# Sigmoid attention in turns of two head pairs, with the last 64 keys of four heads computed in quarters of the PE array

## The chip, the cores and the metric

The kernel runs on one core of a Trainium2 chip. The metric is the device time of one execution in microseconds (us). Before the change three runs took 1089.77, 1091.10 and 1091.86 us; the median is 1091.1 us. The profile shows one more execution, which took 1089.6 us.

## The reference

Three layers run one behind the other. The first is the attention, with a sigmoid in place of the softmax; the change is there alone.

```python
# 1. attention: batch 4, 12 heads, 448 rows, head width 64
scores = (1/sqrt(64)) * (q @ k.T) - log(448)        # 448 x 448 for every head
x = sigmoid(scores) @ v                             # heads side by side: 4 x 448 x 768
# 2. gated layer
h = relu(x @ w_in)                                  # 768 -> 1024
u, v = h[..., :512], h[..., 512:]
v_n = (v - mean(v)) / sqrt(var(v) + 1e-6)
gated = u * (einsum('ts,bsd->btd', w_spatial, v_n) + b_spatial)
x = gated @ w_out                                   # 512 -> 768
# 3. MLP
xn = (x - mean(x)) / sqrt(var(x) + 1e-6) * g_ln
out = x + relu(xn @ w_ch1) @ w_ch2                  # 768 -> 3072 -> 768
```

## The kernel before, in words

**Numbers.** Everything is fp32. Most matmuls take each operand as a high and a low part in the type fp32r and add three products (high with high, high with low, low with high), each of which goes through the PE once. The sums over v in the attention are plain fp32 matmuls instead; each of them shows as two records in the trace.

**Attention.** The 48 heads are taken as 24 pairs. A pair's q and k lie transposed in SBUF, the first head in partitions 0 to 63 and the second in 64 to 127. `qk_load` (L347) fetches them raw, `qk_split` (L363) makes the high and low parts: two casts on the VectorE and two subtractions on GpSimd (the first two pairs aside). A pair has four blocks of 128 keys. The last block has 64 keys of its own: the host repeats the last 64 keys to fill it up to 512 and sets the repeated rows of v to zero, so that half of its work adds nothing. `qk` (L377) computes two blocks of scores: per block six matmuls with 64 rows and 128 columns of the array each, in three twos, one head of the pair in the upper half of the array's rows and the other in the lower half; a block lands in two PSUM banks, one for each head, out of a pool of two such double banks (`ps2`). The ScalarE makes the sigmoid of a block in one instruction (L391). `av` (L394) sums over two blocks: per block two fp32 matmuls, 128 rows and 64 columns of the array each, one head in the left half of the columns, the other in the right half. `x_end` (L407) splits the pair's result into the next layer's operand x (ScalarE copy, VectorE subtraction), and frees the bank.

**The order.** It is written out by hand in the loop of L735. A step is half a pair. Even steps: two blocks of scores (blocks 0 and 1 of pair p), then the sums of the whole pair p-1 (16 records). Odd steps: two blocks of scores (2 and 3), then a stretch of background matmuls worth 2 * BG_US = 4.6 us by the kernel's own costs. The background (`bg`, L724) computes the gated layer's first matmuls `hv` and `hu` for the batches 0 to 2, lines 246 to 248; it does nothing as long as its x or its weights are not there. After each step `jobs.pop` runs one or two jobs of the weight pipeline: `load` of a chunk of w_in (768 KB), `decode` (ScalarE L265, VectorE L266, L267, L270), `split` (ScalarE L276, VectorE L277). There are two raw buffers for chunks, so the load of chunk n+2 waits for the decode of chunk n. All loads go through SyncE's queue in order, but for a few at the start.

**Memory.** Raw q and k have rings of three buffers, their parts rings of two, sigmoids a ring of six. PSUM has the two double banks and four single banks (`ps1`), which the sums and the background share.

**After the attention** w_spatial is loaded (L766) and split (`w_split`, L807), and the last batch's `hv` and `hu`, the spatial matmuls, the projection and the MLP follow.

Of the kernel before, what the change touches and what calls it, by code (L numbers as in the profile page):

```python
# [10 lines left out]
F32 = mybir.dt.float32  # L11
F32R = mybir.dt.float32r
U32 = mybir.dt.uint32
AF = mybir.ActivationFunctionType
ALU = mybir.AluOpType

P = 128
B, H, S, D = 4, 12, 448, 64
NPAIR = H // 2
SK = 512  # L20
DM = H * D
KC = DM // P
DFF = 1024
# [17 lines left out]
BG_US = 2.3  # L41
# [8 lines left out]
VN_DVE = [range(4), range(4), (1, 3), (1, 3)]  # L50
HU_EVERY = 3

PLAIN = range(B * H)

R_SIZE, F_SIZE = 34944, 17664

# [85 lines left out]
class Ring:  # L142
# [61 lines left out]
def sigmoid_attention_gmlp_mlp(ctx: ExitStack, tc, q, k, v, w_in, w_sp, w_out, g_ln, w1, w2, out):  # L204
    nc = tc.nc
# [1 line left out]
    small = ctx.enter_context(tc.tile_pool(name="small", bufs=4))  # L207
    dram = ctx.enter_context(tc.tile_pool(name="dram", bufs=1, space=bass.MemoryType.DRAM))
    ps_s = ctx.enter_context(tc.tile_pool(name="ps_s", bufs=2, space=bass.MemoryType.PSUM))
    ps_1 = ctx.enter_context(tc.tile_pool(name="ps_1", bufs=4, space=bass.MemoryType.PSUM))  # L210

    R = Arena("r", const.tile([P, R_SIZE], F32R, name="r_all"))
    F = Arena("f", const.tile([P, F_SIZE], U32, name="f_all"))
# [6 lines left out]
    bias_s = const.tile([P, 1], F32, name="bias_s")  # L220
# [12 lines left out]

    ctx.enter_context(tc.manual_schedule())

    def ps1():
        return ps_1.tile([P, 512], F32, tag="ps1", name="ps1")

    def ps2():
        return ps_s.tile([P, 2, 512], F32, tag="ps2", name="ps2")  # L240
# [77 lines left out]
    now = [0]  # L318
# [6 lines left out]
    wu = [R.alloc(KC * DH), R.alloc(KC * DH)]  # L325
    xp = [R.alloc(KC * 2 * S), R.alloc(KC * 2 * S)]
    q_r = [Ring(R, S, 2) for _ in range(2)]
    k_r = [Ring(R, SK, 2) for _ in range(2)]
    rv = Ring(F, 512, 3)
    rq = Ring(F, S, 3)  # L330
    rk = Ring(F, SK, 3)
    af_r = Ring(F, 2 * S, 6)
    a_rings = [*q_r, *k_r, rv, rq, rk, af_r]

    n_pairs = B * NPAIR
    pairs = {}
# [9 lines left out]
    @on_pairs  # L346
    def qk_load(p, b, hp):  # L347

        qr, kr = rq.next().ap(S), rk.next().ap(SK)
        pairs[p] = dict(raw=(qr, kr))  # L350
        for j in range(2):
            rows = slice(D * j, D * j + D)
            eng = nc.scalar if p < 3 and j else nc.sync
            eng.dma_start(kr[rows], k[b, hp, :, j])  # L354
            eng.dma_start(qr[rows], q[b, hp, :D, j])

    @on_pairs
    def pv_load(p, b, hp):
        pairs[p]["v"] = rv.next().ap(8, D)
        nc.sync.dma_start(pairs[p]["v"], v[b, hp])  # L360

    @on_pairs
    def qk_split(p, b, hp):  # L363
        t = pairs[p]
        qr, kr = t["raw"]
        (qh, ql), (kh, kl) = ([r.next().ap(n) for r in rs] for rs, n in ((q_r, S), (k_r, SK)))
        t.update(qh=qh, ql=ql, kh=kh, kl=kl)
        eng = nc.gpsimd if p > 1 else nc.vector
        if p:
            nc.vector.tensor_copy(kh, kr)  # L370
        else:
            nc.scalar.copy(kh, kr)
        nc.vector.tensor_copy(qh, qr)
        eng.tensor_sub(kl, kr, kh)  # L374
        eng.tensor_sub(ql, qr, qh)  # L375

    def qk(p, t):  # L377


        a = pairs[p]  # L380
        for c in (2 * t, 2 * t + 1):
# [8 lines left out]
            af = af_r.next().ap(2, S)  # L390
            nc.scalar.activation(af, ps[:, :, :S], AF.Sigmoid, bias=bias_s, scale=1.0 / math.sqrt(D))  # L391
            a["a", c] = af

    def av(p, t):  # L394

        a = pairs[p]
        if t == 0:
            a["ps"] = ps1()
        for c in (2 * t, 2 * t + 1):
            af = a.pop(("a", c))  # L400
            for j in range(2):
                rows = slice(D * j, D * j + D)
                nc.tensor.matmul(  # L403
                    a["ps"][rows, :S], a["v"][:, 4 * j + c], af[:, j], start=(c == 0), stop=(c == 3)
                )
# [41 lines left out]
    def hv(b):  # L447
# [281 lines left out]
    qk_load(1)  # L729
    pv_load(0)  # L730
    qk_split(0)
    qk_load(2)
    pv_load(1)
    jobs.pop(1)
    for i in range(2 * n_pairs):  # L735
        p, t = divmod(i, 2)
        now[0] = i
        qk(p, t)
        if t == 0:
            qk_split(p + 1)  # L740
            qk_load(p + 3)
        else:
            pv_load(p + 2)
        if t:
            bg.run(2 * BG_US)
        elif p:
            av(p - 1, 0)
            av(p - 1, 1)
            x_end(p - 1)
        jobs.pop(0 if i < FIRST else 2 if i >= MORE else 1)  # L750
        if i == WO_FROM:
            c0, c1, c2, c3 = wo_chunks
            for job in (c0.load, c1.load, idle, c0.decode, c1.decode, c2.load, c3.load):
                jobs.add([job, idle])
    now[0] += 1
    av(n_pairs - 1, 0)
    av(n_pairs - 1, 1)
    x_end(n_pairs - 1)
    now[0] = 10**9
    for r in a_rings:  # L760
        r.free()

    wsp_b = R.at(PLACE_WSP, 8 * S)
    wsp = wsp_b.cut(4 * S, 4 * S)
# [157 lines left out]
```

## Time and profile before

| | us |
|---|---|
| median of three runs | 1091.1 (1089.77 to 1091.86) |
| the profiled execution | 1089.6 |
| its span, first to last instruction | 1087.4 |
| PE busy | 1074.3 (99%) |
| VectorE, ScalarE, GpSimd busy | 542.0, 315.6, 104.3 |
| score matmuls L387, 576 records | 73.7 |
| sums L403, 384 records | 77.5 |
| sigmoids L391, 96 | 91.4 |

PE is the matmul part of TensorE, PEld its loading of weights, DVE the VectorE, ACT the ScalarE, POOL GpSimd, SP SyncE (SPq: its issuing of DMAs). A busy time counts overlapping instructions once. Matmul records overlap: the distance from start to start tells what one costs, the length of a record does not. The attention fills the first 247 us.

### The profile page before, as it was taken

How to read it: one execution, taken by the hardware profiler on the slowest of the kernel's cores; microseconds unless marked ns; L12 is line 12 of the kernel's file. 1: busy time of each engine (PE TensorE's matmuls, PEld its weight loads, DVE VectorE, ACT ScalarE, POOL GpSimd, SP SyncE). 2: the span in 40 equal slices, each digit the busy share in tenths (PEclk: the TensorE clock that was granted, in tenths of full speed). 3: DMA queues.
4: the chain of work that ended last, by engine and by line, in shares of the span. 5: the costliest groups of instructions: out<-in, count | busy, mean ns of one | idle time of the engine just before them, and what ended most of it. 6: DMA issues, size and time to landing. Idle time of an engine off the chain costs nothing.

```text
span 1087.4 us, 14037 instructions
## 1 busy us (share of the span) xinstructions
PE 1074.3 (99%) x5860; PEld 877.6 (81%) x5860; DVE 542.0 (50%) x789; ACT 315.6 (29%) x465; POOL 104.3 (10%) x96
## 2 busy tenths in 40 slices
PE   7999999999999999999999999999999999999998
PEld 4466666668888888888888888888888888888887
DVE  4750113205676866364555555463636464555533
ACT  6764445443543432111212121211212111212110
POOL 1232121211215510000000000000000000000000
PEclk9999999999999999999999999999999999999999
DMA  9743335315510112011111112020202011111013
GB/s 244 218 125 96 98 107 173 123 61 189 180 65 1 59 59 88 30 58 58 59 59 58 59 34 83 9 80 30 87 30 87 30 59 58 58 58 58 1 58 145
DMA packets 31951, 87.94 MB, mean 81 GB/s; under 512 B 7568, under 2 KB 12816, under 8 KB 31760
## 3 DMA queue, kind: packets, MB, share of 16 engines
q1 hardware_dynamic: 29808, 78.97, 22.5%
q0 software_dynamic: 1600, 7.34, 2.0%
q8 instruction: 46, 0.75, 0.3%
q10 hardware_dynamic: 480, 0.74, 0.2%
q14 instruction: 17, 0.14, 0.0%
HBM read 74.17 MB, written 12.86 MB: 80 GB/s over the span
## 4 chain that ended last, share of the span: by engine, by line
PE 92%; issue 5%; DMA 1%; POOL 1%; ACT 0%; DVE 0%; SPq 0%; POOLq 0%; DVEq 0%
PE ps L246 27%; PE ps L247 26%; PE ps L248 26%; PE ps L403 6%; PE ps L387 5%; DMA f_all<-in_q 1%; PE ps L597 1%; DMA f_all<-in_k 0%; POOL vnorm L420 0%; POOL r_all L375 0%; PE ps L537 0%; PE ps L536 0%; POOL f_all L778 0%; DVE f_all L539 0%; SPq L354 0%
## 5 line engine op out<-in xcount | busy, mean ns | idle before, releaser
L246 PE MATMUL ps<-r_all 128*128 128x512 f32 (+2 forms) x1588 | 562.9, 354 | 2.3 <-DVE f_all L539 1.1
L247 PE MATMUL ps<-r_all 128*128 128x512 f32 (+2 forms) x1588 | 559.8, 352 | 0.0
L248 PE MATMUL ps<-r_all 128*128 128x512 f32 (+2 forms) x1588 | 557.9, 351 | 0.0
L246 PEld LDWEIGHTS ps<-r_all 128*128 128x128 f32 x1588 | 300.3, 189 | 50.3 <-issue 6.9
L248 PEld LDWEIGHTS ps<-r_all 128*128 128x128 f32 x1588 | 299.7, 189 | 39.4
L247 PEld LDWEIGHTS ps<-r_all 128*128 128x128 f32 x1588 | 300.4, 189 | 37.5
L652 DVE TENSOR_TENSOR f_all<-ps,f_all 128x768 f32<-128x768 f32 (+1 forms) x169 | 161.1, 953 | 164.4 <-PE ps L248 164.3
L634 ACT ACTIVATE r_all<-ps 128x512 fp32r<-128x512 f32 (+1 forms) x96 | 52.0, 542 | 393.2 <-PE ps L248 393.2
L635 DVE SCALAR_TENSOR_TENSOR r_all<-ps,r_all 128x512 fp32r<-128x512 f32 (+1 forms) x96 | 59.7, 622 | 144.5 <-ACT r_all L634 144.5
L391 ACT ACTIVATE f_all<-ps,bias_s 128x896 f32<-128x896 f32 x96 | 91.4, 1003 | 40.0 <-PE ps L387 39.7
L276 ACT CAST r_all<-f_all 128x768 fp32r<-128x768 f32 x60 | 49.8, 834 | 172.5 <-DVE f_all L270 137.1
L277 DVE TENSOR_TENSOR r_all<-ps,r_all 128x384 fp32r<-128x384 f32 (+1 forms) x52 | 29.1, 582 | 127.3 <-ACT r_all L276 127.3
L387 PE MATMUL ps<-r_all 64*128 64x448 f32 x576 | 73.7, 383 | 6.3 <-ACT f_all L391 4.0
L387 PEld LDWEIGHTS ps<-r_all 64*128 64x128 f32 x576 | 50.3, 184 | 36.2 <-issue 20.8
L403 PE MATMUL ps<-f_all 128*64 128x448 f32 x384 | 77.5, 545 | 0.0
L277 DVE TENSOR_TENSOR r_all<-f_all,r_all 128x768 fp32r<-128x768 f32 x60 | 58.0, 970 | 16.2 <-ACT r_all L276 16.2
L267 DVE SCALAR_TENSOR_TENSOR f_all<-f_all 128x768 uint32<-128x768 uint32 x60 | 57.5, 958 | 2.1
L270 DVE SCALAR_TENSOR_TENSOR f_all<-f_all 128x768 uint32<-128x768 uint32 x60 | 57.5, 958 | 2.1
L403 PEld LDWEIGHTS ps<-f_all 128*64 128x64 f32 x384 | 25.4, 136 | 40.9 <-issue 40.0
L265 ACT ACTIVATE f_all<-f_all 128x768 f32<-128x768 f32 x60 | 54.4, 906 | 5.1 <-DVE r_all L277 5.1
L374 POOL TENSOR_TENSOR r_all<-f_all,r_all 128x512 fp32r<-128x512 f32 x22 | 30.1, 1370 | 166.5 <-DVE r_all L370 153.6
L266 DVE TENSOR_SCALAR f_all<-f_all 128x768 uint32<-128x768 uint32 x60 | 33.6, 561 | 7.0 <-ACT f_all L265 7.0
(60 smaller groups left out, 310.2 us busy)
## 6 DMA issues: line engine op xcount, KB each, us to landing
f_all<-in_w SPq DMA_DIRECT2D x48, 768.0 KB, 4.3
f_all<-in_v SPq DMA_DIRECT2D x24, 256.0 KB, 3.0
f_all<-in_w_in SPq DMA_DIRECT2D x8, 768.0 KB, 5.1
f_all<-in_k SPq DMA_DIRECT2D x45, 128.0 KB, 3.1
f_all<-in_q SPq DMA_DIRECT2D x45, 112.0 KB, 3.1
out_y<-f_all SPq DMA_DIRECT2D x13, 384.0 KB, 2.3
vscr<-f_all SPq DMA_DIRECT2D x14, 256.0 KB, 2.0
uscr<-f_all SPq DMA_DIRECT2D x16, 224.0 KB, 2.0
```

The lines of the kernel that those rows point to most:

```text
L246: nc.tensor.matmul(ps, lh, rh, start=first, stop=False)
L247: nc.tensor.matmul(ps, lh, rl, start=False, stop=False)
L248: nc.tensor.matmul(ps, ll, rh, start=False, stop=last)
L265: nc.scalar.mul(f, high.bitcast(F32), 2.0**-112)
L267: nc.vector.scalar_tensor_tensor(bits, low, 29, bits, op0=ALU.logical_shift_right, op1=ALU.bitwise_or)
L270: nc.vector.scalar_tensor_tensor(bits, high, 0x80000000, bits, op0=ALU.bitwise_and, op1=ALU.bitwise_or)
L277: eng.tensor_sub(lo, x, hi)
L387: nc.tensor.matmul(ps[:, j, :S], a[w][rows, kc], a[x][rows], start=(i == 0), stop=(i == 2))
L391: nc.scalar.activation(af, ps[:, :, :S], AF.Sigmoid, bias=bias_s, scale=1.0 / math.sqrt(D))
L403: nc.tensor.matmul(a["ps"][rows, :S], a["v"][:, 4 * j + c], af[:, j], start=(c == 0), stop=(c == 3))
L635: nc.vector.scalar_tensor_tensor(hl[:, f], ps[:, :n], 0.0, hh[:, f], op0=ALU.max, op1=ALU.subtract)
L652: nc.vector.tensor_add(y[:, ws], ps, y[:, ws])
```

## The change

The loop takes two pairs, four heads, in one turn; there are 12 turns. Scores and sums of the first 384 keys stay as they were, three blocks per pair. They come in bursts of two blocks: (p,0) (p,1), then (p,2) (p+1,0), then (p+1,1) (p+1,2). The sums of the odd pair of the turn before and of the even pair of this one stand between the bursts, with 12 records each. The last 64 keys of both pairs are computed apart. `scores_rest` takes the raw fp32 q and k, without parts: four matmuls, one for each head, each in a quarter of the array (64 rows, 64 columns), into one double bank, and one sigmoid for all four heads. One turn later `sums_rest` takes four matmuls in quarters again, two into the bank of the even pair and two into that of the odd pair. The padding to 512 keys goes, and half the work that added nothing with it. Sums have a pool of two banks of their own (`psa`); the background keeps two single banks during the attention and gets the two others after it. A turn has one stretch of background, 4 * BG_US, at its end. Four `beside()` in a turn run the jobs, by the same counter as the steps before. Raw loads for two pairs follow the turn's first burst. In the last turn the raw rings of q and k are freed, and w_spatial is loaded into them.

```diff
+SM = 3 * P
-PLAIN = range(B * H)
+PLAIN = ()
-    ps_1 = ctx.enter_context(tc.tile_pool(name="ps_1", bufs=4, space=bass.MemoryType.PSUM))
+    ps_1 = ctx.enter_context(tc.tile_pool(name="ps_1", bufs=2, space=bass.MemoryType.PSUM))
+    ps_a = ctx.enter_context(tc.tile_pool(name="ps_a", bufs=2, space=bass.MemoryType.PSUM))
...
-    k_r = [Ring(R, SK, 2) for _ in range(2)]
+    k_r = [Ring(R, SM, 2) for _ in range(2)]
-    af_r = Ring(F, 2 * S, 6)
+    af_r = Ring(F, 2 * S, 5)
+    rest_r = Ring(F, 2 * S, 2)
...
+    def scores_rest(p):
+        ps = ps2()
+        for j in range(2):
+            rows = slice(D * j, D * j + D)
+            for i in range(2):
+                qr, kr = pairs[p + i]["raw"]
+                nc.tensor.matmul(
+                    ps[D * i : D * i + D, j, :S], kr[rows, SM:S], qr[rows], start=True, stop=True
+                )
+        pairs[p]["rest"] = sigmoid(rest_r.next().ap(2, S), ps)
+
+    def sums_rest(p):
+        af = pairs[p].pop("rest")
+        pairs[p + 1]["ps"] = psa()
+        for i in range(2):
+            a = pairs[p + i]
+            rows = slice(D * i, D * i + D)
+            for j in range(2):
+                nc.tensor.matmul(
+                    a["ps"][D * j : D * j + D, :S], a["v"][rows, 4 * j + 3], af[rows, j], start=(i == 1), stop=(i == 0)
+                )
...
-    for i in range(2 * n_pairs):
-        p, t = divmod(i, 2)
-        now[0] = i
-        qk(p, t)
-        if t == 0:
-            qk_split(p + 1)
-            qk_load(p + 3)
-        else:
-            pv_load(p + 2)
-        if t:
-            bg.run(2 * BG_US)
-        elif p:
-            av(p - 1, 0)
-            av(p - 1, 1)
-            x_end(p - 1)
...
+    def rests(p):
+        if p < n_pairs:
+            scores_rest(p)
+        if p:
+            sums_rest(p - 2)
+            x_end(p - 2)
+
+    for p in range(0, n_pairs, 2):
+        if p:
+            rests(p)
+            pv_load(p + 1)
+        scores((p, 0), (p, 1))
+        if p:
+            sums(p - 1)
+            x_end(p - 1)
+            pv_load(p + 2)
+        else:
+            rests(p)
+        beside()
+        qk_load(p + 3)
+        qk_load(p + 4)
+        if p + 2 == n_pairs:
+            rq.free()
+            rk.free()
+            wsp_raw = F.alloc(5 * S)
+            nc.sync.dma_start(wsp_raw.ap(5 * S), w_sp)
+        scores((p, 2), (p + 1, 0))
+        beside()
+        sums(p)
+        qk_split(p + 2)
+        beside()
+        scores((p + 1, 1), (p + 1, 2))
+        qk_split(p + 3)
+        beside()
+        bg.run(4 * BG_US)
+    rests(n_pairs)
...
+    sums(n_pairs - 1)
     x_end(n_pairs - 1)
+    singles.append(psa)
```

On the PE, in the middle of the attention, a pair of before stands like this between two stretches of background (L387 scores, L403 sums, L246 the background):

```order
L387 MATMUL ps_826<-r_all 128x448 x6
L387 MATMUL ps_834<-r_all 128x448 x6
L403 MATMUL ps_850<-f_all 64x448 x8
L387 MATMUL ps_861<-r_all 128x448 x6
L387 MATMUL ps_869<-r_all 128x448 x6
L246 MATMUL ps_878<-r_all 128x448
```

After the change a turn of two pairs stands there (L412 scores in quarters, L426 sums in quarters, L399 scores, L439 sums, L253 the background):

```order
L412 MATMUL ps_625<-f_all 64x448 x4
L426 MATMUL psa<-f_all 64x448 x4
L399 MATMUL ps_639<-r_all 128x448 x6
L399 MATMUL ps_647<-r_all 128x448 x6
L439 MATMUL psa<-f_all 64x448 x6
L399 MATMUL ps_672<-r_all 128x448 x6
L399 MATMUL ps_680<-r_all 128x448 x6
L439 MATMUL psa<-f_all 64x448 x6
L399 MATMUL ps_699<-r_all 128x448 x6
L399 MATMUL ps_707<-r_all 128x448 x6
L253 MATMUL ps_621<-r_all 128x448
```

Two pairs had eight blocks of scores and 16 program matmuls of sums; they have six blocks and 12, and eight quarters in a row.

On the ScalarE, at the start, where weights are still decoded, the end of pair 3 and the start of pair 4 stood like this before (L391 sigmoids, L265 decode, L276 split of a chunk):

```order
L391 ACTIVATE f_all<-ps_328,bias_s 128x896
L391 ACTIVATE f_all<-ps_336,bias_s 128x896
L265 ACTIVATE f_all<-f_all 128x768
L276 CAST r_all<-f_all 128x768
L391 ACTIVATE f_all<-ps_354,bias_s 128x896
```

After the change the same place, between the turn of pairs 2 and 3 and that of pairs 4 and 5, reads (L386 sigmoids, the third of them that of the quarters, L272 decode, L283 a split):

```order
L386 ACTIVATE f_all<-ps_307,bias_s 128x896
L386 ACTIVATE f_all<-ps_315,bias_s 128x896
L272 ACTIVATE f_all<-f_all 128x768
L283 CAST r_all<-f_all 128x768
L386 ACTIVATE f_all<-ps_336,bias_s 128x896
L283 CAST r_all<-psa 128x448
L386 ACTIVATE f_all<-ps_350,bias_s 128x896
```

The decode and the split of a chunk still stand ahead of the next pair's first sigmoid, which now is that of the quarters.

## Rows read from the trace of the kernel before

**Rows 1.** Busy time in three stretches: us, then each engine, clock, DMA share.
```profile
0.00:57.00 57.00, 49.66 (x300) 27.35 (x301) 33.82 (x56) 39.45 (x48) 13.90 (x15) 1.00 0.83 234
57.00:246.00 189.00, 189.00 (x1071) 124.77 (x1073) 41.34 (x82) 91.36 (x114) 43.72 (x36) 1.00 0.36 109
246.00:300.00 54.00, 51.75 (x243) 44.06 (x240) 33.91 (x59) 24.72 (x41) 11.39 (x15) 1.00 0.57 191
```
**Rows 2.** PE in order of time, one pair: start us, us, line, form, count.
```profile
126.76 1.50 PE L387 MATMUL ps<-r_all 64*128 64x448 f32 x12
128.18 3.23 PE L403 MATMUL ps<-f_all 128*64 128x448 f32 x16
131.34 1.49 PE L387 MATMUL ps<-r_all 64*128 64x448 f32 x12
132.76 0.50 PE L246 MATMUL ps<-r_all 128*128 128x512 f32 x1
133.09 0.40 PE L247 MATMUL ps<-r_all 128*128 128x512 f32 x1
...
137.21 0.39 PE L247 MATMUL ps<-r_all 128*128 128x512 f32 x1
137.44 0.39 PE L248 MATMUL ps<-r_all 128*128 128x512 f32 x1
137.76 1.50 PE L387 MATMUL ps<-r_all 64*128 64x448 f32 x12
```
**Rows 3.** All engines in order of time, about the first sums of that pair.
```profile
127.74 1.91 ACT L391 ACTIVATE f_all<-ps,bias_s 128x896 f32<-128x896 f32 x2 [0.95 <-PE ps L387]
...
128.18 1.35 PE L403 MATMUL ps<-f_all 128*64 128x448 f32 x6
...
128.61 0.14 PEld L403 LDWEIGHTS ps<-f_all 128*64 128x64 f32 x2 [0.23 <-issue]
128.99 0.14 PEld L403 LDWEIGHTS ps<-f_all 128*64 128x64 f32 x2 [0.23 <-issue]
```
**Rows 4.** All engines in order of time, the first block of its scores.
```profile
126.18 0.60 ACT L464 ACTIVATE f_all<-ps 128x512 f32<-128x512 f32 x1 [3.11 <-PE ps L248]
...
126.76 0.88 PE L387 MATMUL ps<-r_all 64*128 64x448 f32 x6
```
**Rows 5.** The page's groups: count | busy us, mean ns | idle before.
```profile
L391 ACT ACTIVATE f_all<-ps,bias_s 128x896 f32<-128x896 f32 x96 | 91.4, 1003 | 40.0 <-PE ps L387 39.7
L387 PE MATMUL ps<-r_all 64*128 64x448 f32 x576 | 73.7, 383 | 6.3 <-ACT f_all L391 4.0
L267 DVE SCALAR_TENSOR_TENSOR f_all<-f_all 128x768 uint32<-128x768 uint32 x60 | 57.5, 958 | 2.1
L270 DVE SCALAR_TENSOR_TENSOR f_all<-f_all 128x768 uint32<-128x768 uint32 x60 | 57.5, 958 | 2.1
L265 ACT ACTIVATE f_all<-f_all 128x768 f32<-128x768 f32 x60 | 54.4, 906 | 5.1 <-DVE r_all L277 5.1
L266 DVE TENSOR_SCALAR f_all<-f_all 128x768 uint32<-128x768 uint32 x60 | 33.6, 561 | 7.0 <-ACT f_all L265 7.0
```
**Rows 6.** PE in order of time, the start: idle time before in brackets.
```profile
6.20 2.12 PE L387 MATMUL ps<-r_all 64*128 64x448 f32 x12 [0.94 <-DVE r_all L373]
...
18.05 1.77 PE L387 MATMUL ps<-r_all 64*128 64x448 f32 x12 [0.91 <-ACT f_all L391]
...
26.03 1.77 PE L387 MATMUL ps<-r_all 64*128 64x448 f32 x12 [1.65 <-ACT f_all L391]
```
**Rows 7.** Busy time in stretches of 5 us at the start.
```profile
10.00:15.00 5.00, 4.75 (x32) 2.23 (x32) 0.82 (x2) 3.56 (x4) 1.52 (x2) 1.00 1.05 272
15.00:20.00 5.00, 4.07 (x30) 2.21 (x28) 3.41 (x6) 4.08 (x6) 0.91 (x1) 1.00 1.04 284
```
**Rows 8.** DMA issues of the first 30 us: KB each, us to landing.
```profile
f_all<-in_w_in SPq DMA_DIRECT2D x4, 768.0 KB, 7.3
```
**Rows 9.** ScalarE in order of time, behind the attention.
```profile
256.03 1.69 ACT L811 CAST r_all<-f_all 128x1792 fp32r<-128x1792 f32 x1 [8.02 <-DMA f_all<-in_w_sp]
```

More of the change, by code (lines that the diff above doesn't have):

```diff
@@ L19 @@
 NPAIR = H // 2
-SK = 512
+SM = 3 * P
 DM = H * D
@@ L234, in sigmoid_attention_gmlp_mlp, with psa @@
     ctx.enter_context(tc.manual_schedule())
+    def psa():
+        return ps_a.tile([P, 512], F32, tag="psa", name="psa")
+    singles = [lambda: ps_1.tile([P, 512], F32, tag="ps1", name="ps1")]
     def ps1():
-        return ps_1.tile([P, 512], F32, tag="ps1", name="ps1")
+        singles.append(singles.pop(0))
+        return singles[-1]()
     def ps2():
@@ L327, in sigmoid_attention_gmlp_mlp @@
     q_r = [Ring(R, S, 2) for _ in range(2)]
-    k_r = [Ring(R, SK, 2) for _ in range(2)]
+    k_r = [Ring(R, SM, 2) for _ in range(2)]
     rv = Ring(F, 512, 3)
+    af_r = Ring(F, 2 * S, 5)
+    rest_r = Ring(F, 2 * S, 2)
     rq = Ring(F, S, 3)
-    rk = Ring(F, SK, 3)
-    af_r = Ring(F, 2 * S, 6)
-    a_rings = [*q_r, *k_r, rv, rq, rk, af_r]
+    rk = Ring(F, S, 3)
+    a_rings = [*q_r, *k_r, rv, af_r, rest_r]
     n_pairs = B * NPAIR
@@ L347, in qk_load @@
     def qk_load(p, b, hp):
-        qr, kr = rq.next().ap(S), rk.next().ap(SK)
+        qr, kr = rq.next().ap(S), rk.next().ap(S)
         pairs[p] = dict(raw=(qr, kr))
@@ L353, in qk_load @@
             eng = nc.scalar if p < 3 and j else nc.sync
-            eng.dma_start(kr[rows], k[b, hp, :, j])
+            eng.dma_start(kr[rows], k[b, hp, :, j, :S])
             eng.dma_start(qr[rows], q[b, hp, :D, j])
@@ L365, in qk_split @@
         qr, kr = t["raw"]
-        (qh, ql), (kh, kl) = ([r.next().ap(n) for r in rs] for rs, n in ((q_r, S), (k_r, SK)))
+        (qh, ql), (kh, kl) = ([r.next().ap(n) for r in rs] for rs, n in ((q_r, S), (k_r, SM)))
         t.update(qh=qh, ql=ql, kh=kh, kl=kl)
@@ L369, in qk_split, with sigmoid, scores @@
         if p:
-            nc.vector.tensor_copy(kh, kr)
+            nc.vector.tensor_copy(kh, kr[:, :SM])
         else:
-            nc.scalar.copy(kh, kr)
+            nc.scalar.copy(kh, kr[:, :SM])
         nc.vector.tensor_copy(qh, qr)
-        eng.tensor_sub(kl, kr, kh)
+        eng.tensor_sub(kl, kr[:, :SM], kh)
         eng.tensor_sub(ql, qr, qh)
-    def qk(p, t):
-        a = pairs[p]
-        for c in (2 * t, 2 * t + 1):
+    def sigmoid(af, ps):
+        nc.scalar.activation(af, ps[:, :, :S], AF.Sigmoid, bias=bias_s, scale=1.0 / math.sqrt(D))
+        return af
+    def scores(*blocks):
+        for p, c in blocks:
+            a = pairs[p]
             ps = ps2()
@@ L389, in qk, with sums @@
                     )
[L390 to L394, printed above, removed]
+            a["a", c] = sigmoid(af_r.next().ap(2, S), ps)
+    def scores_rest(p):
[18 more added lines that the diff above has]
+                )
+    def sums(p):
         a = pairs[p]
-        if t == 0:
-            a["ps"] = ps1()
-        for c in (2 * t, 2 * t + 1):
+        if p % 2 == 0:
+            a["ps"] = psa()
+        for c in range(3):
             af = a.pop(("a", c))
@@ L403, in av @@
                 nc.tensor.matmul(
-                    a["ps"][rows, :S], a["v"][:, 4 * j + c], af[:, j], start=(c == 0), stop=(c == 3)
+                    a["ps"][rows, :S],
+                    a["v"][:, 4 * j + c],
+                    af[:, j],
+                    start=(p % 2 == 0 and c == 0),
+                    stop=(p % 2 == 1 and c == 2),
                 )
@@ L729, in sigmoid_attention_gmlp_mlp, with beside @@
     qk_load(1)
+    qk_split(0)
+    qk_split(1)
     pv_load(0)
-    qk_split(0)
     qk_load(2)
     pv_load(1)
+    pv_load(2)
     jobs.pop(1)
-    for i in range(2 * n_pairs):
-        p, t = divmod(i, 2)
-        now[0] = i
-        qk(p, t)
-        if t == 0:
-            qk_split(p + 1)
-            qk_load(p + 3)
-        else:
-            pv_load(p + 2)
-        if t:
-            bg.run(2 * BG_US)
-        elif p:
-            av(p - 1, 0)
-            av(p - 1, 1)
-            x_end(p - 1)
+    step = iter(range(10**9))
+    def beside():
+        i = now[0] = next(step)
         jobs.pop(0 if i < FIRST else 2 if i >= MORE else 1)
@@ L754, in sigmoid_attention_gmlp_mlp @@
                 jobs.add([job, idle])
+    def rests(p):
[33 more added lines that the diff above has]
+    rests(n_pairs)
     now[0] += 1
-    av(n_pairs - 1, 0)
-    av(n_pairs - 1, 1)
+    sums(n_pairs - 1)
     x_end(n_pairs - 1)
+    singles.append(psa)
     now[0] = 10**9
@@ L764, in sigmoid_attention_gmlp_mlp @@
     wsp = wsp_b.cut(4 * S, 4 * S)
-    wsp_raw = F.alloc(5 * S)
-    nc.sync.dma_start(wsp_raw.ap(5 * S), w_sp)
     vraw_r = Ring(F, 4 * DH, 2)
```

## The prediction

> **What bounds the kernel now.** I read the stretches first [rows 1]. Between 57 and 246 us the PE is busy for 189.00 of 189.00 us at a granted clock of 1.00: in three quarters of the attention nothing but the PE counts, and a microsecond taken from its queue is a microsecond of the kernel. Before 57 us it is busy for 49.66 us, so 7.3 us are idle; between 246 and 300 us 2.25 us are. ScalarE has half of the middle stretch free (91.36 of 189), VectorE more, and DMA works at 0.36 there. So I price the change in PE time first, and look for new waits second. The length of a matmul record says little (they overlap), so all prices are distances from start to start in one pair's timeline [rows 2].
>
> **The PE's prices.** A burst of two score blocks takes from 126.76 to 128.18 and from 131.34 to 132.76, 1.42 us each. The sums of four blocks, 16 records, take from 128.18 to 131.34, 3.16 us. The records go two at a time: weight loads come in twos at 128.61 and 128.99, and six records end 1.35 us after the first start, sixteen 3.23 us after it, so a further two cost (3.23 - 1.35) / 5 = 0.376 us [rows 2, 3]. One two is thus a "slot" of 0.376 us. Going to the background and back costs a little: the last background matmul is followed after 0.32 us (137.44 to 137.76) where 0.23 is normal (137.21 to 137.44), and the first of the next stretch by 0.33 (132.76 to 133.09), so 0.09 + 0.10 = 0.19 us [rows 2]. A pair's attention is 1.42 + 3.16 + 1.42 + 0.19 = 6.19 us; two pairs are 12.38.
>
> **A turn after.** Three score bursts are 3 x 1.42 = 4.26. Two bursts of sums with 12 records are 2 x (3.16 - 2 x 0.376) = 4.82. One round trip to the background is 0.19. New are eight fp32 matmuls in quarters, four for scores and four for sums, in one array shape and so without a change of shape between them. No row shows a quarter. The nearest rows are halves: the score records use half of the rows and start in twos, the sums use half of the columns and start in twos [rows 2, 3]. If upper and lower rows, and left and right columns, are independent together as they are one by one, four quarters run at once; four matmuls of two records each are then two slots, and scores and sums of the rest four slots: a burst of sums with 8 records, 3.16 - 4 x 0.376 = 1.66. If only two go at once it is eight slots, 3.16; one at a time, sixteen, 3.16 + 8 x 0.376 = 6.17. Less than 1.66 is excluded, since the two records of a quarter follow each other and a slot is what one of them takes. I take 1.66, because both directions of sharing are seen in the rows and the four results of a step go to different halves of two banks, as in L387 and L403. The turn is 4.26 + 4.82 + 0.19 + 1.66 = 10.93, that is 1.45 less, and over 12 turns 17.4 us less.
>
> **What could wait in the middle.** The rest's scores borrow one of the two double banks, so the second block of each turn waits for the rest's sigmoid. Scores of the rest end 0.97 us after the turn starts (as four records in [rows 3] would: 1.35 - 0.376); a sigmoid starts 0.10 us after its matmuls (126.76 + 0.88 to 127.74) and takes 1.00, so the bank is free at 2.07 [rows 3 to 5]. The PE wants it at 1.66 + half a burst, 2.37. It fits with 0.3 us; if a background eviction of 0.60 us [rows 4] happens to stand in front, up to 0.3 us of waiting a turn comes, 3 us in all; usually the eviction is over by then, and I cost it at nothing. The third block of a burst of sums needs the sigmoid of a block that was computed 0.71 us before the sums began: 0.10 + 1.00 - 0.71 = 0.4 us into them, while the first two blocks give 1.5 us of cover. Two single banks instead of four for the background: a tile fills in 18 x 0.23 = 4.1 us and is evicted in 0.60, so nothing, unless ScalarE hangs. Behind each wait on the PE stands the whole queue, so these covers matter. The PE has more waits on DMAs (each quarter of scores names its own q and k loads), but those loads were issued a turn before, some 20 us. SyncE issues the raw loads of two pairs in one go, eight DMAs, and that queue has nothing urgent behind it in the middle. ScalarE loses 12 sigmoids of 1.00 us and GpSimd and VectorE split 384 columns instead of 512; none of them is on the path.
>
> **The start.** Here the change can cost. Less PE time per pair does not make loads faster, and DMA is full from 10 to 20 us (1.05 and 1.04 of its capacity, 272 and 284 GB/s) [rows 7]. The second turn begins with the quarters of pairs 2 and 3, so it needs q and k of four pairs (4 x 448 KB), three v (256 KB) and, ahead of pair 3 in the queue, a chunk (768 KB): 3.4 MB, at 275 GB/s 12.4 us behind the first issue, plus issue and landing some 17 us. Without waits the PE would be there at 15: 2 us. Next, the weight pipeline. With two raw buffers, two chunks take one load and one decode, 7.3 us [rows 8] + 0.91 on ScalarE + 0.56 + 2 x 0.96 on VectorE [rows 5], 10.7 us; a turn runs eight jobs, 8/3 chunks, so 14.3 us. In the second and third turn, that have little background yet, the PE asks for 10.9. The decode stands in ScalarE's queue ahead of the quarters' sigmoid, and so holds the PE through the bank. Against 14.3, 12.4 for two pairs now is also short, and the 1.65 us wait at 26.03 is of that kind [rows 6]; the extra is at most 2 x (12.38 - 10.93) = 2.9 us, at least 0 (a later load lands sooner when DMA is not full). I take 1. The 0.91 us wait at 18.05 [rows 6] goes into the new ones. Together + 2 us, with bounds of - 3 (the order happens to remove waits) and + 6.
>
> **The end.** w_spatial's load now starts a turn earlier; today ScalarE stands 8.02 us for it behind the attention [rows 9]. The PE does not: it has the last batch's matmuls, and idles 2.25 us in that stretch in all [rows 1]. So the gain lies between 0 and 2.25; I take 1, the nearer part of the waits being evictions that the ScalarE's backlog delays.
>
> **Sum.** The profiled execution took 1089.6 us: 1089.6 - 17.4 + 2 - 1 = 1073.2. The median of the runs lies 1.5 us above that execution, so I forecast 1074.7 us.
>
> **Rivals.**
>
> 1. *Strict order of the halves (slower).* Each fp32 matmul is two records. If the PE starts records strictly in program order and the two of one matmul stand next to each other, the second half of one quarter goes ahead of the first half of the next; it can start only when its own quarter is free, and all behind it wait. Only the second half of one and the first half of the next overlap: eight matmuls take nine slots, 3.16 + 0.376 = 3.54, and the change costs 12 x (3.54 - 1.66) = 22.6 us more: 1097. It decides from 1.66 + 1.45 = 3.11 us for the rest, that is from eight slots on. Against it: the sums of today have the same two records a matmul, and would show a lone first and last slot, nine slots for 16 records; sixteen records take 3.16 us, eight slots and a bit, and weights are loaded in twos [rows 2, 3]. For it: no row shows a third partner.
>
>    The Trainium skill ("TensorE: Matmul & The Clock Gate", Part 3, The mechanism) states that matmuls start and end in strict program order, without reordering. If the two halves of an fp32 matmul are two such matmuls, its rule gives this rival's 1097; the trace does not agree with that reading for halves of columns, where the starts come in twos. The same part (Measured speedup vs the span model) gives 10.6 times for sixteen small tiles over rows and columns at once; by that the rest is four slots and the sum stays as forecast. No run here shows either for quarters.
>
> 2. *Two at a time (no change).* Rows and columns cannot be shared at once, or the streams of four quarters are too many; eight slots, 12 x (3.16 - 1.66) = 18.0 us more: 1092.7. For it: no four-way row exists. Against: in L403 each partition already feeds two streams, and a quarter asks no more of it.
>
> 3. *The start eats more (faster by less).* Loads and decodes pace the first three turns at the upper bound, and the rest's sigmoid stands behind evictions: + 4 and + 3, some 1080. For it: DMA at 1.05 [rows 7]. Against: the loads run ahead by a turn.
>
> That the last 64 keys do not shrink is excluded by the order: 4 + 4 + 36 + 12 program matmuls a turn stand where 48 + 16 stood.
>
> **How the numbers follow.** Forecast 0.72, rival 3 0.11, rival 2 0.08, rival 1 with all that is slower still (up to 6.17 a rest, 1129) 0.09. A measurement of this kernel tells 0.2% (2.2 us) from no change. Faster is the forecast and rival 3, 0.83; rival 2 lies mostly within 0.2%, 0.06; the remainder, 0.11, is slower. The range for 8 in 10 goes from 1068 (start - 3, end - 2.25, little else) to 1086 (rival 3, and the rest at six slots instead of four, 9 us).
>
> **What would show it.** Right: the records of L412 start in fours, the rest (first L412 to first L399) takes near 1.7 us, L399 bursts stay at 1.42 and L439 at 2.4, the middle stretch stays at 100% busy, and the attention ends near 230 us instead of 247. Wrong: a rest of 3 us or more (rivals 1 and 2); idle time of the PE before 57 us well over 9 us (rival 3); waits of L399 on L386 in the middle turns.

## The result and the profile after

Four runs of the changed kernel took 1078.66 to 1082.90 us, median 1080.66, against 1091.34 before (four runs, one more than at first): ratio 0.9905, 95% interval 0.9886 to 0.9924. The forecast was 1074.7 us within 1068 to 1086: the sign and the range held, but of the forecast gain of 16.4 us 10.7 came. The profiled execution took 1082.9 us (span 1080.7).

First the middle, where the gain was to come from. PE in order of time, one turn of two pairs, from the last background matmul of one stretch to the first of the next; it answers to [rows 2]:

```profile
140.64 0.39 PE L255 MATMUL ps<-r_all 128*128 128x512 f32 x1
140.96 0.98 PE L412 MATMUL ps<-f_all 64*64 64x448 f32 x8
141.76 0.93 PE L426 MATMUL psa<-f_all 64*64 64x448 f32 x8
142.62 1.49 PE L399 MATMUL ps<-r_all 64*128 64x448 f32 x12
...
144.04 2.48 PE L439 MATMUL psa<-f_all 128*64 128x448 f32 x12
146.45 1.48 PE L399 MATMUL ps<-r_all 64*128 64x448 f32 x12
147.86 2.48 PE L439 MATMUL psa<-f_all 128*64 128x448 f32 x12
150.27 1.49 PE L399 MATMUL ps<-r_all 64*128 64x448 f32 x12
...
151.68 0.50 PE L253 MATMUL ps<-r_all 128*128 128x512 f32 x1
```

From the first quarter to the first full block are 142.62 - 140.96 = 1.66 us, the price that was forecast for four at once. Bursts of scores still take 1.42 (142.62 to 144.04), sums 2.41 (144.04 to 146.45). The turn's attention takes 10.72 us (140.96 to 151.68) and 0.19 for the background's border: 10.91, against 10.93 forecast. From the first quarter to the first full block all eight turns from the fifth on take 1.66. All engines at the start of the same turn show the fours, as [rows 3] showed the twos:

```profile
140.96 0.21 PEld L412 LDWEIGHTS ps<-f_all 64*64 64x64 f32 x8 [0.35 <-issue]
...
141.38 0.15 PEld L426 LDWEIGHTS psa<-f_all 64*64 64x64 f32 x4 [0.22 <-issue]
...
141.76 0.15 PEld L426 LDWEIGHTS psa<-f_all 64*64 64x64 f32 x4 [0.22 <-issue]
142.08 1.01 ACT L386 ACTIVATE f_all<-ps,bias_s 128x896 f32<-128x896 f32 x1 [1.10 <-PE ps L412]
```

Weights come in fours, 0.38 us apart, one slot; the sigmoid of the rest starts 1.12 us after the turn does (forecast 1.07).

So the loss lies elsewhere. Busy time in stretches, columns as in [rows 1] (us, then PE, PEld, DVE, ACT, POOL, granted clock, DMA share, GB/s):

```profile
0.00:57.00 57.00, 45.63 (x262) 25.48 (x262) 33.54 (x50) 33.09 (x41) 13.46 (x16) 0.94 0.70 208
57.00:230.00 173.00, 170.84 (x990) 110.36 (x992) 46.08 (x85) 81.07 (x105) 36.59 (x33) 0.98 0.39 122
230.00:300.00 70.00, 70.00 (x348) 58.79 (x345) 44.32 (x81) 37.90 (x64) 14.17 (x20) 1.00 0.50 169
```

From 230 us on, through the end of the attention at 244.0 us, the PE idles no more (2.25 us before). At the start it idles 11.4 + 2.2 us where it idled 7.3, and the clock is no longer 1.00. PE in order of time with its waits (in brackets) there:

```profile
19.01 1.82 PE L412 MATMUL ps<-f_all 64*64 64x448 f32 x8 [3.56 <-ACT f_all L386]
...
24.03 2.48 PE L439 MATMUL psa<-f_all 128*64 128x448 f32 x12
...
38.12 0.48 PE L399 MATMUL ps<-r_all 64*128 64x448 f32 x2 [1.34 <-POOL r_all L383]
39.68 1.15 PE L399 MATMUL ps<-r_all 64*128 64x448 f32 x6 [1.09 <-ACT f_all L386]
40.76 3.82 PE L439 MATMUL psa<-f_all 128*64 128x448 f32 x12
...
58.03 1.49 PE L399 MATMUL ps<-r_all 64*128 64x448 f32 x6 [2.60 <-ACT f_all L386]
59.45 4.71 PE L439 MATMUL psa<-f_all 128*64 128x448 f32 x12
```

The same 12 sums take 2.48, 3.82 and 4.71 us: at 19.6, 40.1 and 57.2 us, each time in or just behind a wait or a group of waits, the PE falls to the lower of its two clock levels, 1.2 GHz, for a while. Three windows, each within one such while (clock: the figure before the DMA share):

```profile
19.70:23.00 3.30, 3.30 (x18) 1.79 (x12) 2.07 (x4) 1.69 (x3) 2.01 (x2) 0.50 0.86 284
...
40.20:43.50 3.30, 3.30 (x12) 1.01 (x12) 3.27 (x4) 1.68 (x2) 0.65 (x1) 0.50 0.02 5
...
57.20:63.90 6.70, 5.87 (x18) 2.07 (x18) 3.50 (x4) 3.12 (x4) 0.64 (x1) 0.50 0.23 93
```

12.5 busy us at half the clock are some 6.2 us lost. The books nearly close: 12 x (12.38 - 10.91) = 17.6 gained in the turns, 2.25 at the end; against them 6.2 more idle time at the start and 6.2 from the clock. That leaves some 7.5, and the spans differ by 6.7.

What made the PE wait? ScalarE in order of time:

```profile
17.17 0.89 ACT L272 ACTIVATE f_all<-f_all 128x768 f32<-128x768 f32 x1 [4.49 <-DMA f_all<-in_w_in]
17.96 1.89 ACT L386 ACTIVATE f_all<-ps,bias_s 128x896 f32<-128x896 f32 x2
...
56.19 0.89 ACT L272 ACTIVATE f_all<-f_all 128x768 f32<-128x768 f32 x1 [2.62 <-DMA f_all<-in_w_in]
56.98 1.00 ACT L386 ACTIVATE f_all<-ps,bias_s 128x896 f32<-128x896 f32 x1
```

ScalarE stands for a chunk of w_in with sigmoids queued behind; the PE waits for their double bank. And SyncE's queue in order of time, with its waits within the lengths, and at the end its largest wait up to 72 us (line, releaser, us in total, times, longest):

```profile
32.03 3.19 SPq L264 DMA_DIRECT2D f_all<-in_w_in  x2
35.75 9.21 SPq L368 DMA_DIRECT2D f_all<-in_v  x2
45.13 0.33 SPq L264 DMA_DIRECT2D f_all<-in_w_in  x1
...
50.94 3.91 SPq L264 DMA_DIRECT2D f_all<-in_w_in  x2
...
SPq L368 <- PE psa L439: 21.5, 3, 8.8
```

The two v loads hold the queue for 9.2 us, the second because the sums still read its buffer. The chunk behind them starts at 45 us, the q and k of the next turn after it, and the chunk after those at 50.94; by the order of the loads it is the one that ScalarE waits for until 56.19.

### The profile page after: what moved, and what is told of

Its sections match the earlier page's. It is cut to its first block, busy times and chain, and to the rows that moved or that the text cites. A ratio compares the mean times of both kernels' runs of the same rounds, so it can differ in the third digit from the quotient of the medians.

```text
span 1080.7 us, 13972 instructions
## 1 busy us (share of the span) xinstructions
PE 1063.7 (98%) x5812; PEld 869.9 (80%) x5812; DVE 547.9 (51%) x789; ACT 305.0 (28%) x453; POOL 97.9 (9%) x96
## 4 chain that ended last, share of the span: by engine, by line
PE 95%; DMA 2%; ACT 1%; DVE 1%; SPq 0%; issue 0%; DVEq 0%; ACTq 0%
PE ps L253 22%; PE ps L254 22%; PE ps L255 21%; PE psa L254 6%; PE psa L253 6%; PE psa L255 6%; PE psa L439 5%; PE ps L399 4%; DMA f_all<-in_w_in 2%; PE ps L412 1%; PE psa L426 1%; DMA f_all<-in_v 0%; ACT f_all L272 0%; PE ps L637 0%; PE psa L637 0%; ACT f_all L386 0%
## 5 line engine op out<-in xcount | busy, mean ns | idle before, releaser
L253 PE MATMUL ps<-r_all 128*128 128x512 f32 (+2 forms) x1250 | 438.6, 351 | 0.0
L254 PE MATMUL ps<-r_all 128*128 128x512 f32 (+2 forms) x1250 | 436.9, 350 | 0.0
L255 PE MATMUL ps<-r_all 128*128 128x512 f32 (+2 forms) x1250 | 435.1, 348 | 0.0
L253 PEld LDWEIGHTS ps<-r_all 128*128 128x128 f32 x1250 | 236.6, 189 | 34.4 <-issue 4.1
L255 PEld LDWEIGHTS ps<-r_all 128*128 128x128 f32 x1250 | 236.0, 189 | 29.9
L254 PEld LDWEIGHTS ps<-r_all 128*128 128x128 f32 x1250 | 236.7, 189 | 28.4
L692 DVE TENSOR_TENSOR f_all<-ps,f_all 128x768 f32<-128x768 f32 x168 | 160.7, 957 | 164.3 <-PE ps L255 164.3
L253 PE MATMUL psa<-r_all 128*128 128x512 f32 (+2 forms) x338 | 122.9, 364 | 0.0
L255 PE MATMUL psa<-r_all 128*128 128x512 f32 (+2 forms) x338 | 122.8, 363 | 0.0
L254 PE MATMUL psa<-r_all 128*128 128x512 f32 (+2 forms) x338 | 122.8, 363 | 0.0
L674 ACT ACTIVATE r_all<-ps 128x512 fp32r<-128x512 f32 (+1 forms) x48 | 26.0, 542 | 275.6 <-PE ps L255 275.6
L283 ACT CAST r_all<-f_all 128x768 fp32r<-128x768 f32 x60 | 49.9, 834 | 169.9 <-DVE f_all L277 134.4
L386 ACT ACTIVATE f_all<-ps,bias_s 128x896 f32<-128x896 f32 x84 | 80.9, 1005 | 41.8 <-PE ps L399 21.2
L675 DVE SCALAR_TENSOR_TENSOR r_all<-psa,r_all 128x512 fp32r<-128x512 f32 (+1 forms) x48 | 29.9, 623 | 90.3 <-ACT r_all L674 90.3
L284 DVE TENSOR_TENSOR r_all<-psa,r_all 128x448 fp32r<-128x448 f32 (+1 forms) x38 | 22.6, 596 | 97.8 <-ACT r_all L283 97.8
L253 PEld LDWEIGHTS psa<-r_all 128*128 128x128 f32 x338 | 63.8, 189 | 9.4
L255 PEld LDWEIGHTS psa<-r_all 128*128 128x128 f32 x338 | 63.8, 189 | 9.4
L254 PEld LDWEIGHTS psa<-r_all 128*128 128x128 f32 x338 | 63.8, 189 | 9.4
L399 PEld LDWEIGHTS ps<-r_all 64*128 64x128 f32 x432 | 38.3, 188 | 36.0 <-issue 18.7
L284 DVE TENSOR_TENSOR r_all<-f_all,r_all 128x768 fp32r<-128x768 f32 x60 | 57.8, 965 | 16.3 <-ACT r_all L283 16.2
L439 PE MATMUL psa<-f_all 128*64 128x448 f32 x288 | 63.4, 576 | 1.1 <-ACT f_all L386 1.1
L399 PE MATMUL ps<-r_all 64*128 64x448 f32 x432 | 56.5, 390 | 5.6 <-ACT f_all L386 4.0
```

The lines of the kernel that those rows point to most:

```text
L253: nc.tensor.matmul(ps, lh, rh, start=first, stop=False)
L254: nc.tensor.matmul(ps, lh, rl, start=False, stop=False)
L255: nc.tensor.matmul(ps, ll, rh, start=False, stop=last)
L399: nc.tensor.matmul(ps[:, j, :S], a[w][rows, kc], a[x][rows], start=(i == 0), stop=(i == 2))
L439: nc.tensor.matmul(a["ps"][rows, :S], a["v"][:, 4 * j + c], af[:, j], start=(p % 2 == 0 and c == 0), stop=(p % 2 == 1 and c == 2),)
L674: nc.scalar.activation(hh[:, f], ps[:, :n], AF.Relu)
```

## The experiments

All times are medians; the ratio is to the kernel before, from runs on the same chip. For the changed kernel it is 0.9905 (0.9886 to 0.9924). The theory was that the loss has one cause, the weight pipeline's decodes in ScalarE's queue ahead of sigmoids, with late chunks behind v loads, and the clock following the waits. The rivals: the clock falls because of the quarters; the start is bound by DMA, whatever the order.

**e1_fill: dummy work in the first wait.**

```diff
...
     def rests(p):
+        if p == 2:
+            pairs[p - 1]["ps"] = psa()
+            for _ in range(14):
+                nc.tensor.matmul(pairs[p - 1]["ps"][:, :P], warm, warm, start=True, stop=True)
```

> The changed kernel with 14 matmuls of the warm-up kind (128x128 fp32, zeros, their results overwritten) put ahead of the quarters of pairs 2 and 3, where the PE stands idle for 3.56 us; they need some 3.0 us at full clock. Theory: the stretch at half clock from 19.6 to 23.0 us follows from that idle time. Then it goes, the quarters at 19 us run at 1.00, and the time falls by about 3.4/2 = 1.7 us to 1079; the two later stretches at half clock (40.1 and 57.2 us) stay. Rival: the half clock belongs to the quarters themselves (the new, smaller matmuls) and not to the idle time; then the stretch stays although the PE was busy, and the time stays at 1080.7.

1079.93 us, 0.9908 (0.9893 to 0.9923). Two windows, the wait and what follows, and the 12 sums that had taken 3.82 us at 40.76:

```profile
14.00:19.00 5.00, 5.00 (x46) 4.45 (x48) 1.82 (x3) 2.70 (x3) 0.00 (x0) 1.00 0.72 157
19.70:23.00 3.30, 3.30 (x31) 1.54 (x22) 1.15 (x3) 3.06 (x4) 2.20 (x2) 1.00 0.97 333
...
38.27 2.48 PE L440 MATMUL psa<-f_all 128*64 128x448 f32 x12
```

With the PE busy the clock stays at 1.00 behind it, with the same quarters. So the quarters by themselves don't lower the clock. Against the expectation the second stretch at half clock went too in this execution, though the waits ahead of it stayed (1.34 and 1.08 us). The median moved by 0.7 us, less than the runs spread: the later waits stayed, and the one before the fourth turn grew from 0.62 to 2.36 us.

**e2_v4 and e3_c0: the order of loads.**

```diff
-    rv = Ring(F, 512, 3)
+    rv = Ring(F, 512, 4)          # e2_v4
...
     pv_load(1)
-    pv_load(2)
     jobs.pop(1)                   # the first chunk of w_in
+    pv_load(2)                    # e3_c0
```

> The changed kernel with four buffers for raw v instead of three. Theory: SyncE's queue is held by the v loads, which wait for the sums that still read the buffer (21.5 us in three waits, 8.8 the longest), and the chunks of w_in and the next q and k stand behind; so chunks land late, ScalarE waits for them with the sigmoids queued behind. Without those waits of SyncE the later chunks land some us earlier, the PE's waits at 37 to 40 us and at 52 to 58 us (5.7 us together) shrink to 1 or 2, and the half clock behind them goes (5 us): 1073 to 1076. Rival: the start is bound by what DMA can move, or by ScalarE's work alone, and the order of the queue makes no difference: 1080 to 1081 with the same waits.

> The changed kernel with the first chunk of w_in loaded ahead of pair 2's v, as before the change. Theory: the chunk is issued 1.5 to 2.5 us earlier and lands near 15 instead of 17.15 us, its decode stops holding the sigmoids of pair 1, the PE's wait of 3.56 us at 19 us falls to about 1.5 and the first stretch at half clock goes: 1.7 + 2 less, 1077. Rival: q and k of pair 3, which the quarters need too, land just as late (DMA is full there), so the wait is only renamed: 1080 to 1081.

e2_v4: 1076.30, 0.9873 (0.9859 to 0.9886), a clear gain of some 4 us. e3_c0: 1080.00, 0.9903 (0.9890 to 0.9917): a miss, at its rival's figure. Its first wait fell from 3.56 to 2.70 us only; the half clock behind it went, but the wait before the fourth turn grew from 0.62 to 2.67. In e2_v4 SyncE's waits of the v loads for the sums are gone (21.5 us in the changed kernel), and the buffers of the chunks are first:

```profile
SPq L264 <- DVE f_all L277: 16.6, 5, 6.4
SPq L506 <- ACT f_all L504: 10.9, 2, 7.4
```

The queue's order is a part of the cause, not all of it; the PE still waited 1 to 3 us in six places. Its idle time fell by only 1.8 us in the profiled executions (13.5 to 11.7); much of the gain is the clock, at a mean of 0.997 or 0.998 instead of 0.994 to 0.997.

**e5_more16: half the pace of the weight pipeline.**

```diff
-FIRST, MORE = 1, 4
+FIRST, MORE = 1, 16
```

> The changed kernel with one job of the weight pipeline per place instead of two until place 16, so one and a third chunks a turn instead of two and two thirds. Theory: from 25 us on the PE waits because decode and split stand ahead of sigmoids in ScalarE's queue; at half the pace the waits at 33 to 40 and 52 to 68 us (7.8 us) go nearly all, with two stretches at half clock behind them (5 us); the background begins a turn later, and what it loses runs behind the attention at no cost: 1070 to 1074. Rival: the waits come from q, k and v, and the late background leaves the PE without cover: no gain or a loss, 1080 to 1084.

1072.74, 0.9852 (0.9831 to 0.9874), with two of five runs at 1075.7 and 1078.8. Two windows, where the waits had been and where the pace doubles again:

```profile
25.00:57.00 32.00, 32.00 (x212) 16.03 (x214) 24.31 (x31) 25.43 (x31) 11.24 (x10) 1.00 0.66 201
75.70:82.40 6.70, 4.54 (x11) 3.59 (x12) 6.34 (x9) 2.49 (x4) 2.89 (x2) 0.50 0.21 78
```

The largest single step of all: 8 us by the medians, 6 by the means. Where two jobs a place come back a new wait appears, its longest, and ScalarE shows what is ahead:

```profile
PE ps L253 <- ACT f_all L504: 4.4, 1, 4.4
...
72.97 0.89 ACT L272 ACTIVATE f_all<-f_all 128x768 f32<-128x768 f32 x1 [4.14 <-DVE r_all L284]
```

A background tile waits 4.4 us for an eviction (L504) that stands behind a decode (L272), two sigmoids and two splits in ScalarE's queue; the decode itself had waited 4.14 us for a split's subtraction on the VectorE (L284), and not for a chunk as the expectation of e6_pace has it. That four single banks would have covered it is argued, not shown.

The window with 32.00 of 32.00 busy us hides a wait, too: the quarters that start at 55.28 take 3.17 us instead of 1.66, as their weight loads wait twice for k (0.60 and 0.42 us).

**e6_pace and e7_before_pace: one job a place all through, in the changed kernel (with four buffers for v) and in the kernel before.**

```diff
-FIRST, MORE = 1, 4
+FIRST, MORE = 1, 10**9
```

> The changed kernel with one job of the weight pipeline per place all through, and four buffers for raw v. With one job until place 16 the PE was busy for 32.00 of 32 us between 25 and 57 us, but when two jobs came again it stood once for 4.4 us (a background matmul waiting for an eviction, behind a decode that waited for a chunk), with 6.8 us of half clock behind. Theory: both go, and what is left is the wait of some 2.5 us before the second turn: 1089.6 - 17.4 (the turns) - 2.2 (no idle time behind the attention) - 1 (start) = 1069, 1068 to 1071. Rival: the two single banks of the background are too few whatever the pace, and the wait moves elsewhere: 1073 or more.

> The kernel before with the same slower pace of the weight pipeline (one job a step all through). Theory: before, the PE is slow enough that the pace costs little; of its 7.3 us idle at the start the waits behind decodes (about 3) may go: 1087 to 1091. Rival: the pace is the whole of the gain and the turns and quarters bring nothing by themselves; then it falls as far as the changed kernel does with that pace, to 1075 or less.

e6_pace: 1073.03, 0.9832 (0.9811 to 0.9854). The 4.4 us wait went. One of its runs took 1068.13 us at a mean clock of 1.000, the lower end of the theory's range; the three others took 1072.9 to 1074.1 at 0.996 or 0.997, near the rival's figure, though the rival's wait isn't there: the clock accounts for some 3 to 4 of the 5 to 6 us between them. e7_before_pace: 1089.60, 0.9991 (0.9982 to 0.9999): the pace alone gives the kernel before next to nothing. It is the faster PE that made the old pace too quick.

**e8_norest: the quarters left out.**

```diff
...
     def rests(p):
-        if p < n_pairs:
-            scores_rest(p)
         if p:
-            sums_rest(p - 2)
             x_end(p - 2)
```

> The changed kernel with the slower pace and four buffers for v, and the last 64 keys left out of scores, sigmoids and sums. It measures what the quarters cost. Theory: 12 turns at 1.66 us, four quarters at once: 20 us less than with them (1049), a little more where the first turns wait for pair 3's loads. Rival, two quarters at a time: 12 x 3.16 = 38 us less (1031).

1060.21, 0.9721 (0.9708 to 0.9735): 12.8 us less than e6_pace, not 20. A steady turn, from its first score to the background, and the largest waits:

```profile
113.94 1.50 PE L399 MATMUL ps<-r_all 64*128 64x448 f32 x12
...
123.01 0.50 PE L253 MATMUL ps<-r_all 128*128 128x512 f32 x1
...
PE ps L399 <- ACT f_all L386: 4.3, 2, 3.8
PE ps L399 <- POOL r_all L383: 3.1, 3, 1.3
PE ps L399 <- DVE r_all L381: 3.1, 3, 2.0
```

The steady turn takes 9.07 us (113.94 to 123.01) where the changed kernel's takes 10.72: 1.65 less, so the quarters cost there what they were priced at. The total does not show it, because with yet less PE work the start waits for splits and sigmoids again (some 3 us more than in e6_pace), and the mean clock is 0.994 or 0.995 (in e6_pace 0.996 or 0.997 in most runs). A price of 3.16, 38 us less, is far away.

**e9_wsp: w_spatial loaded behind the attention again, in e6_pace.**

```diff
-            wsp_raw = F.alloc(5 * S)
-            nc.sync.dma_start(wsp_raw.ap(5 * S), w_sp)
...
     wsp = wsp_b.cut(4 * S, 4 * S)
+    wsp_raw = F.alloc(5 * S)
+    nc.sync.dma_start(wsp_raw.ap(5 * S), w_sp)
```

> The changed kernel with the slower pace and four buffers for v, and w_spatial loaded behind the attention again. It measures what the early load brings. Theory: ScalarE stands 8 us for the load, the evictions and splits pile up behind, and the PE loses the 1 to 2.25 us again that it lost before the change: 1 to 2 us more than with the early load. Rival: the PE's idle time there came from the attention's end (evictions after the last sums), and w_spatial brings nothing: the same within 0.5 us.

1072.15, 0.9839 (0.9826 to 0.9853): the same as with the early load, as its rival had it. ScalarE, in order of time, waits for it again, and the PE does not notice:

```profile
229.79 1.69 ACT L877 CAST r_all<-f_all 128x1792 fp32r<-128x1792 f32 x1 [4.56 <-DMA f_all<-in_w_sp]
```

and busy time from 230 us on, columns as above:

```profile
230.00:300.00 70.00, 70.00 (x338) 63.07 (x337) 49.91 (x96) 36.31 (x70) 10.27 (x14) 1.00 0.48 165
```

**e11_pace_fill, e10_c0, e12_all: toward the best version.** e11 is e6_pace with 13 dummies in the first wait. e10 is e6_pace with the first chunk ahead of v 2 and its decode a place later (FIRST = 2). e12 is e10 with 9 dummies.

> The changed kernel with the slower pace, four buffers for v, and 13 dummy matmuls ahead of the quarters of pairs 2 and 3, where the PE still waits 2.7 to 3.7 us. Theory: the runs at that pace differ by the clock alone (1068.1 at a mean clock of 1.000, 1073 at 0.997), and the clock falls behind that one wait; with the wait filled no run falls, and all lie at 1068 to 1069. Rival: the clock falls by chance or by the quarters, and the runs spread from 1068 to 1074 as without the dummies.

> The changed kernel with the slower pace, four buffers for v, the first chunk of w_in loaded ahead of pair 2's v, and its decode one place later, behind the sigmoids of pair 1. Theory: the wait before the second turn falls from 2.7 to 3.7 us to under 1.5, since ScalarE no longer holds the sigmoids for the chunk; what is left is the landing of pair 3's q and k. 1066 to 1069, with the clock up in most runs. Rival: the landing of pair 3 is just as late (DMA is full), the wait stays at 2.5 us: 1068 to 1073.

> The kernel of e10_c0 with 9 dummy matmuls ahead of the quarters of pairs 2 and 3. Theory: waits and clock both kept, the fastest of all: 1066 to 1068 in every run. Rival: where the wait is already short the dummies cost up to 1.9 us: 1068 to 1070.

e11: 1071.01, 0.9817 (0.9803 to 0.9831). The spread shrank to 1070.1 to 1072.7, but the clock still fell in most runs, so the one wait that was filled isn't all that lowers it. In the profiled run it fell at 91.6 us, just behind a wait of 1.33 us (the 12 sums take 3.87 us there instead of 2.48):

```profile
90.91 1.31 PE L399 MATMUL ps<-r_all 64*128 64x448 f32 x8 [1.33 <-POOL r_all L383]
92.15 3.87 PE L440 MATMUL psa<-f_all 128*64 128x448 f32 x12
```

e10: 1070.36, 0.9810 (0.9796 to 0.9823). Its second turn starts at 16.16 us and then stands in the middle of the quarters for the q and k of pair 3, the landing that the forecast had priced at 2 us:

```profile
16.16 0.96 PE L412 MATMUL ps<-f_all 64*64 64x448 f32 x2 [0.49 <-ACT f_all L386]
18.61 1.37 PE L412 MATMUL ps<-f_all 64*64 64x448 f32 x5 [1.49 <-DMA f_all<-in_q]
...
21.04 1.49 PE L399 MATMUL ps<-r_all 64*128 64x448 f32 x12
```

The quarters take 4.88 us (16.16 to 21.04) instead of 1.66, so the landing costs some 3 us, more than the 1.49 that show as idle time of the PE.

e12: 1069.77, 0.9803 (0.9790 to 0.9817), 1069.43 to 1070.09 in its runs, all with a mean clock of 1.000. It beats the kernel before and the changed one (by 10.9 us); of e10 it is not clearly apart. The expectations of all three were 1 to 2 us too low, and e10 and e12 ended within their rivals' ranges. For e10 the late landing above is the reason; what e12's dummies cost was not isolated.

**e13_turns: the turns without the quarters.**

```diff
-SM = 3 * P
+SM = 4 * P
...
         scores((p, 0), (p, 1))
         sums(p - 1)
-        scores((p, 2), (p + 1, 0))
-        sums(p)
-        scores((p + 1, 1), (p + 1, 2))
+        scores((p, 2), (p, 3))
+        sums(p, (0, 1))
+        scores((p + 1, 0), (p + 1, 1))
+        sums(p, (2, 3))
+        scores((p + 1, 2), (p + 1, 3))
...
```

> The turns of two pairs with four full blocks of keys per pair again (no quarters, padding kept), a bank for each pair's sums, the slower pace, four buffers for v and the loads of e10_c0, w_spatial loaded behind the attention. The sums of the even pair stand in two halves of 8 records, so that ScalarE keeps up. By the prices of the timeline a turn takes 4 x 1.42 + 3.16 + 2 x 1.66 + 0.19 = 12.35 us against 12.38 for two pairs before. Theory: the quarters are the whole gain of the steady turns, and this runs with the kernel before, 1086 to 1091 (some us for the end and a smoother start). Rival: the order of the turns brings a part of the gain by itself, 1080 or less.

1084.84, 0.9947 (0.9933 to 0.9960). Slightly under the theory's range: some 5 us come from the smoother start and end (54.00 of 54 us busy behind the attention), none from the steady turns, whose bursts cost what they did:

```profile
146.84 3.23 PE L438 MATMUL psa<-f_all 128*64 128x448 f32 x16
149.99 1.49 PE L398 MATMUL ps<-r_all 64*128 64x448 f32 x12
151.41 1.72 PE L438 MATMUL psa<-f_all 128*64 128x448 f32 x8
153.06 1.48 PE L398 MATMUL ps<-r_all 64*128 64x448 f32 x12
```

From here to e10, which adds the quarters (and loads w_spatial early, worth nothing by e9_wsp), are 14.5 us. The turns alone bring little, the quarters the rest.

## Why the prediction was right in its mechanism and too high in its gain

- *The turn, 12.38 to 10.93 us.* Right: 10.91. Four quarters share the array, and four times two records take two slots. Rivals 1 and 2 fall: the trace has all four first halves together, with weights in fours at 141.38 and 141.76. The trace does not agree with the reading of the strict order in the Trainium skill ("TensorE: Matmul & The Clock Gate", Part 3, The mechanism) by which the second half of one quarter would go ahead of the first half of the next.
- *Covers in the middle.* Right: past 70 us no wait of the PE in the attention. The rest's sigmoid fits. The attention ends at 244.0 us, though, not near 230: the 12.4 us lost at the start stand ahead of it. That two single banks cost nothing "unless ScalarE hangs" held with its exception: in e5_more16 it hung, for 4.4 us.
- *The end, - 1.* The idle time went wholly (2.25), but not by w_spatial's early load: e9_wsp idles none either. What removed it was not isolated; e13_turns, without the quarters, has none as well.
- *The start, + 2, with bounds of - 3 and + 6.* This is the term that failed. It measured 6.2 us of idle time, at the upper bound, and 6.2 us of half clock, for which the sum had no price at all. The prediction's own sign of rival 3 showed, 11.4 us idle before 57 us where it named 9. The mechanism of rival 3 was the real one for the start (decodes ahead of sigmoids, e5_more16), and its "some 1080" is where the kernel landed; that the figure fits is partly luck, since its waits behind evictions in the middle did not come and the clock took their place. Two things were missed. The pace was compared with the PE's 10.9 us a turn as if a late chunk cost its own delay; in fact SyncE's in-order queue passed it on to later chunks through v loads (9.2 us, e2_v4), and the second, third and fourth turn started 14.9 and 18.8 us apart (19.01, 33.93 and 52.72; 2.2 of the 18.8 are background), against the 14.3 of the pace. And waits of 1 to 3.6 us were priced by their length, while behind them the PE ran at 1.2 GHz.
- *The first wait.* The 2 us for pair 3's landing were right in kind and too low: it costs some 3 us in e10_c0, where little else is in front.

The range held with a margin made for something else: its upper end counts rests at six slots, which did not come. The two terms it names also add up to more than 1086, some 1080 + 9 = 1089.

What stays open: which waits lower the clock. 1.65 us at 26.03 [rows 6] did not, 1.33 us in e11 did; before the second turn 2.73 us in e2_v4 did not and 2.45 in e5_more16 did; and the same kernel's runs differ in it.

## What to carry to other kernels

Price a shorter stretch of PE work twice: by the work, and by what fed that stretch at the old pace. When the PE gets faster, everything that was timed to it (here a pipeline of jobs popped so many a step) becomes too quick for its own loads, and an in-order queue hands the delay to work that is urgent. Slowing the side work to half its pace was worth 6 to 8 of the 10.9 us that were left. And when K and M are both 64, four fp32 matmuls in quarters of the array, into two banks, cost here what two in halves cost: 1.66 us for eight of them, 1.65 for four in halves (e13_turns). Last, a busy PE can hide a wait inside a burst: compare the burst's length with its steady one.

## What the runs showed of the hardware that was not expected

Idle time on the PE of 1.3 to 4.4 us was followed, not every time, by some 3 to 7 us at 1.2 GHz although the PE was then fully busy (3.30 of 3.30 us). That is the larger part of what makes runs of the same program differ: e6_pace took 1068.1 us at a mean clock of 1.000 and 1073 us at 0.997, e5_more16 1072.1 at 0.998 and 1078.8 at 0.993. Dummy matmuls in the wait kept the clock at no cost that shows (e1_fill: 1.00 behind it), and with the waits shortened too every run agreed within 0.7 us (e12_all).
